# Scores and sign bits in fp16 halves for three of four batches, theta's product in fp16, and a new order of issue

## The chip, the cores and the metric

One core of one Trainium2 chip runs the whole program. The metric is the device time of one execution in microseconds. Seven engines or queues matter below: TensorE (PE, with its weight loads PEld), VectorE (DVE), ScalarE (ACT), GpSimd (POOL) and the SyncE queue (SP), which issues every DMA.

## The reference

Attention over 4 batches, 8 heads, 768 tokens and head size 64, with a mask from random projections, and a mixing layer on its output:

```python
q_bits = (q @ proj > 0); k_bits = (k @ proj > 0)          # 6 bits a token
mask   = bucket(q_bits)[:, None] == bucket(k_bits)[None, :]
scores = where(mask, q @ k.T / 8, -1e9)
x      = softmax(scores) @ v                              # heads side by side: 4 x 768 x 512
theta  = x @ w_theta                                      # 512 x 512
y      = w_tok_r @ (x * cos(theta)) + w_tok_i @ (x * sin(theta))   # 768 x 768, over tokens
u      = x + y
out    = u + max(u @ w_ch, 0)
```

Everything is asked for in float32. A product on TensorE reads operands with fewer bits, so each operand is written as a high part and a low part and a product is three matmuls (high by high, high by low, low by high).

## The kernel before, in words

**Pairs and steps.** Two heads of a batch form a pair; there are 16 pairs, 4 a batch. A pair is prepared once (`prep_qk`, line 601) and then gone through in 6 steps of 128 queries (`step`, line 687), so 24 steps a batch and 96 in all. When the heads of batch b are through, `moe(b, ...)` does the mixing layer of that batch, while the steps of batch b+1 run.

**Preparing a pair.** Queries and keys (`nat`, 128 rows by 768, two buffers, line 614) are loaded by DMA. ACT copies them to `hl` as fp32r (line 621, op `qkh`); DVE or POOL takes the low part by a subtraction (line 628, `qkl`). TensorE multiplies them with the projections `pst` (`bits`, line 642: four matmuls of 512 columns, four of 256), ACT and DVE add up (lines 655, 658), DVE or POOL turns the sums into plus or minus 2^40 (line 661, `sign`), and three DMAs spread the sign rows into `rows` and `kb` (line 673).

**A step.** `scores` (line 696) sums, for each of two heads, three products of `hl` halves and one of the sign rows into PSUM: 8 matmuls a head, each over 64 rows of the array, 4 of 512 columns and 4 of 256. In batches 1 to 3 the two heads' matmuls alternate, one on the array's upper and one on its lower rows (`st`); in batch 0 the heads go one by one. DVE takes the row maximum (line 722) and two small values (725, 728), ACT the exponential `pf` (732), ACT its fp16 copy (738), POOL the fp16 low part (744, `p2`), a DMA on SP transposes both (748), and TensorE multiplies with v (`pv`, 18 matmuls a head). In batch 0, one head of each two is instead transposed on TensorE (772) and multiplied in fp32 (`pv4`). There are two PSUM slots for scores, and one step takes both.

**The mixing layer.** For each of 6 token tiles of a batch: transpose (872), high part on ACT (877), low part on DVE (881), theta's product in fp32r (`project`, 4 times three matmuls of 512 columns), ACT and DVE for its fraction of a turn (913, 916, 919), sine and cosine on ACT (938, 939), then f, z high and z low (950, 955 or 957, 961) on DVE, ACT and POOL. Then 6 times 36 fp16 matmuls of 512 columns (`y`), and again transpose, split and product with `w_ch` in fp32r (`r`).

**Weights.** The weights come in as float64 and are narrowed on DVE, ACT and POOL; `split_weight` (430) makes the fp32r halves of w_theta and w_ch, `prep_wtok` the fp16 halves of the token matrices, `join_wtok` (495) brings their maxima to all partitions by a transpose and a matmul.

**Order.** Every operation is an `op` with a priority, the engines it may run on with a duration for each, its dependencies and its buffer slots. `issue_all` (127) goes through a model of the engines and writes out one fixed order for each engine. Where the model sees TensorE idle before its time 190 us, it puts in a matmul on constants (`fill`, 342). Priorities come from the numbers at the end of the file (KX, KY, W0, QK0 and so on). On the chip each engine then works through its list in order.

**Maxima of v.** `prep_v` already finds a power of two for v in each pair: maximum over the free axis on DVE (547), a DMA that turns the column into a row (550), a maximum of it (553), a DMA that spreads it (556), three small operations for the power of two (389 to 391), and a scaled fp16 copy on ACT (573) with the low part on DVE (582).

Of the kernel before, what the change touches and what calls it, by code (L numbers as in the profile page):

```python
# [31 lines left out]
def lsh_attention_moe_kernel(ctx: ExitStack, tc: tile.TileContext, qk, wt, v, consts, w_theta, w_ch, out):  # L32
# [86 lines left out]
    FREE = dict(nat=2, vr=1, wst=2, vv=2, x=2, z0=1, z1=1, xt=2, **BUFS, s=2, w=1, m=4)  # L119
# [262 lines left out]
    wth = [wp.tile([P, NC, DM], F32R, name=f"wth{i}") for i in range(2)]  # L382
# [5 lines left out]
    def pow2_scale(amax, inv, s):  # L388
        DVE.tensor_scalar(inv, amax, 1e-30, 2.0**-13, ALU.max, ALU.mult)
# [38 lines left out]
    wst_last = []  # L428

# [65 lines left out]
    def join_wtok(prio):  # L495
        t = {}
        sa = Slot("m")

        def own():
            DVE.tensor_reduce(wall, wam, AX.X, ALU.max)  # L500

        def tr():
            t["pa"] = bank(sa, [P, 2, P], "pa_w")
            PE.transpose(t["pa"][:1, 0], wall, ident)

        def row():
            t["a1"] = ap_.tile([1, 1], F32, tag="a1" + sa.tag, bufs=1, name="a1_w")
            DVE.tensor_reduce(t["a1"], t["pa"][:1, 0], AX.X, ALU.max)

        def everywhere():  # L510
            mm(t["pa"][:, 1, :2], t["a1"].to_broadcast([1, P]), ones1, True, True)
# [7 lines left out]
        o = op("wall", prio, on("DVE", 110, own), wamax)  # L519
        o = op("vall", prio, on("PE", 110, tr), [o], [sa])  # L520
        o = op("vall", prio, on("DVE", 198, row), [o], [sa])
        o = op("vall", prio, on("PE", 308, everywhere), [o], [sa])
# [73 lines left out]

# [90 lines left out]
    def step(g, b, hp, i, t, vt, po):  # L687
# [23 lines left out]
        for j in range(2):  # L711
            def head(j=j):
# [14 lines left out]
                def shift():  # L727
                    DVE.tensor_scalar(col(2), col(0), SHIFT, col(1), ALU.add, ALU.mult)  # L728
# [309 lines left out]
SEP = 24  # L1038
# [107 lines left out]
```

## Time and profile before

| | |
|---|---|
| runs shown | 787.96, 790.18, 927.24 us, median 790.18 us |
| profiled execution | 790.58 us, its span 788.8 us, granted clock 0.995 |
| PE busy | 757.3 us (96%), 6881 matmuls |
| DVE busy | 571.3 us (72%) |
| ACT busy | 535.4 us (68%) |
| POOL busy | 427.1 us (54%) |
| mean share of the DMA engines | 64.5% |
| chain that ended last | PE 71%, DVE 12%, ACT 8%, issue 4%, DMA 3% |

The span goes from the first to the last instruction; 1.8 us of the execution lie around it. Matmuls overlap and the end of each is modelled, so what a matmul costs is read from the distance of starts, not from its duration. A chain of waits is followed back from the end of a stretch: at each instruction to what released it, or to the one before it on its engine.

### The profile page before, as it was taken

The numbers are of one execution on the slowest core, as the hardware profiler recorded it, in microseconds if no ns is written. First come the engines' busy times: TensorE is split into PE (matmuls) and PEld (weight loads), VectorE is DVE, ScalarE is ACT, GpSimd is POOL, SyncE is SP. The second block draws the span as 40 slices with busy tenths as digits, with TensorE's granted clock in tenths as the row PEclk, the third lists the DMA queues.
The fourth block names the chain that finished last, engine by engine and source line by source line (L and its number), as shares of the span: only waits on it lengthen the run. The fifth ranks groups of instructions, "written<-read, shape, count | busy, mean of one in ns | idle before, by whom it ended". The sixth has DMA issues, their size and how long they took to land.

```text
span 788.8 us, 17523 instructions
## 1 busy us (share of the span) xinstructions
PE 757.3 (96%) x6881; PEld 537.5 (68%) x6881; DVE 571.3 (72%) x1218; ACT 535.4 (68%) x709; POOL 427.1 (54%) x309
## 2 busy tenths in 40 slices
PE   7999999999798999999999999999999999999998
PEld 3778878788565666777756666677666666666456
DVE  5887878888888787687996666787995665546223
ACT  3796867778898676668996666569966655658101
POOL 5465552646678586455666666465574654433200
PEclk9999999999989999999999999999999999999999
DMA  6357757666556898889349899784489876750002
GB/s 206 114 128 199 153 155 162 165 146 138 100 98 147 173 186 160 188 173 169 73 87 197 174 181 182 156 174 102 83 164 175 143 152 132 147 105 1 0 1 81
DMA packets 285283, 107.84 MB, mean 137 GB/s; under 512 B 270288, under 2 KB 274384, under 8 KB 285200
## 3 DMA queue, kind: packets, MB, share of 16 engines
q1 hardware_dynamic: 285200, 106.71, 64.1%
q8 instruction: 54, 0.88, 0.4%
q14 instruction: 29, 0.24, 0.1%
HBM read 32.54 MB, written 6.29 MB: 49 GB/s over the span
## 4 chain that ended last, share of the span: by engine, by line
PE 71%; DVE 12%; ACT 8%; issue 4%; DMA 3%; POOL 1%; SPq 0%; ACTq 0%; DVEq 0%; POOLq 0%
PE ps L84 67%; DVE mc L722 4%; ACT pf L732 2%; PE ps L772 2%; PE ps L872 2%; ACT pp L738 2%; DMA pt<-pp 1%; DMA nat<-in_qk_dram 1%; DVE rows L661 1%; ACT L732 1%; ACT z L955 1%; ACT n L913 1%; DMA wst<-in_wt_dram 1%; DVE sum L658 1%; DVE z L961 1%
## 5 line engine op out<-in xcount | busy, mean ns | idle before, releaser
L744 POOL TENSOR_TENSOR pp<-pf,pp 128x768 f16<-128x768 f32 x168 | 283.0, 1699 | 213.3 <-ACT pp L738 167.5
L732 ACT ACTIVATE pf<-ps,mc 128x768 f32<-128x768 f32 x192 | 182.5, 988 | 124.3 <-DVE mc L728 100.2
L722 DVE TENSOR_REDUCE mc<-ps 128x1 f32<-128x768 f32 x192 | 177.3, 951 | 91.6 <-PE ps L84 88.3
L84 PE MATMUL ps<-z,wtk 128*128 128x512 f16 x864 | 204.0, 379 | 0.1
L84 PE MATMUL ps<-hl 64*128 64x512 f32 (+1 forms) x1152 | 184.0, 354 | 9.6 <-ACT pf L732 9.5
L84 PEld LDWEIGHTS ps<-hl 64*128 64x128 f32 x1152 | 124.2, 186 | 56.5 <-ACT pf L732 26.8
L84 PE MATMUL ps<-vv,pt 128*128 128x65 f16 (+2 forms) x3312 | 155.0, 201 | 2.5 <-DMA pt<-pp 1.6
L738 ACT ACTIVATE pp<-pf 128x768 f16<-128x768 f32 x168 | 134.5, 839 | 0.5
L84 PEld LDWEIGHTS <-wtk 128*128 128x128 f16 x864 | 77.5, 98 | 79.8 <-issue 1.3
L84 PEld LDWEIGHTS <-pt 128*128 128x128 f16 x3024 | 105.9, 97 | 31.3 <-issue 11.3
L84 PE MATMUL ps<-kb,rows 64*128 64x256 f32 (+1 forms) x384 | 89.8, 335 | 0.0
L961 POOL TENSOR_TENSOR z<-f,z 128x512 f16<-128x512 f32 x31 | 41.0, 1330 | 50.1 <-ACT z L955 31.6
L84 PE MATMUL ps<-wch,h_u 128*128 128x512 f32 x192 | 66.2, 426 | 0.3
L84 PE MATMUL ps<-wth,h_x 128*128 128x512 f32 x192 | 63.3, 411 | 0.9 <-DVE wall L514 0.5
L84 PEld LDWEIGHTS ps<-kb,rows 64*128 64x128 f32 x384 | 53.0, 186 | 5.2
L950 DVE SCALAR_TENSOR_TENSOR f<-x,zr,z 128x512 f32<-128x512 f32 x48 | 46.6, 997 | 7.1 <-ACT z L938 4.9
L877 ACT ACTIVATE h_u<-ps 128x512 fp32r<-128x512 f32 x24 | 14.2, 594 | 51.1 <-PE ps L872 46.8
L84 PEld LDWEIGHTS ps<-wch,h_u 128*128 128x128 f32 x192 | 34.8, 189 | 9.4 <-ACT h_u L877 0.5
L84 PE MATMUL ps<-wch,l_u 128*128 128x512 f32 x96 | 38.2, 398 | 2.9 <-DVE l_u L881 2.9
L84 PEld LDWEIGHTS ps<-wth,h_x 128*128 128x128 f32 x192 | 34.8, 192 | 8.7 <-DVE l_x L881 0.8
L84 PE MATMUL ps<-wth,l_x 128*128 128x512 f32 x96 | 38.5, 401 | 0.6 <-DVE l_x L881 0.6
L84 PE MATMUL ps<-idle 128*128 128x512 f16 x126 | 33.7, 403 | 4.8 <-DVE sum L658 3.3
(115 smaller groups left out, 962.0 us busy)
## 6 DMA issues: line engine op xcount, KB each, us to landing
nat<-in_qk_dram SPq DMA_DIRECT2D x32, 384.0 KB
wst<-in_wt_dram SPq DMA_DIRECT2D x12, 768.0 KB
vb<-in_v_dram SPq DMA_DIRECT2D x16, 384.0 KB
out_dram<-x SPq DMA_DIRECT2D x24, 256.0 KB
pt<-pp SPq DMA_TRANSPOSE x168
w_th<-in_moe_w_theta_dram SPq DMA_DIRECT2D x4, 512.0 KB
w_ch<-in_moe_w_ch_dram SPq DMA_DIRECT2D x8, 256.0 KB
kb<-rows SPq DMA_DIRECT2D x32, 36.0 KB
```

The lines of the kernel that those rows point to most:

```text
L84: PE.matmul(out_, l, r, start=start, stop=stop, skip_group_check=True)
L658: DVE.tensor_tensor(u["s"], u["pb"][:56, :n_], u["s"], ALU.subtract)
L661: return lambda: eng.tensor_scalar(t["rows"][:56, lo : lo + n_], u["s"], affs[:56, 0:1], affs[:56, 1:2], ALU.is_ge, ALU.mult)
L722: DVE.tensor_reduce(col(0), st[j], AX.X, ALU.max, negate=True)
L732: ACT.activation(u["pf"], st[j], AF.Exp, bias=col(2), scale=col(1))
L738: ACT.activation(u["pp"][:, 0], u["pf"], AF.Copy)
L744: return lambda: eng.tensor_tensor(u["pp"][:, 1], u["pf"], u["pp"][:, 0], ALU.subtract)
L772: PE.transpose(u["pw"][:, tt], u["pf"][:, ts(tt, P)], ident)
L872: PE.transpose(u["pt"][:, c], src()[:, c * P : (c + 1) * P], ident)
L877: ACT.activation(u["hi"], u["pt"], AF.Copy)
L950: DVE.scalar_tensor_tensor(u["f"], tl[b][:, tt], t["zr"][:, 2 * tt + r : 2 * tt + r + 1], t["zw"][r][:, tt], ALU.mult, ALU.mult)
L961: return lambda: eng.tensor_tensor(t["z"][r, 1][:, tt], u["f"], t["z"][r, 0][:, tt], ALU.subtract)
```

## The change

In batches 1 to 3 queries and keys are scaled by a power of two and kept as fp16 halves, as are the projections and the sign rows; theta's product takes x and w_theta as scaled fp16 halves in all batches. The scale of a pair comes from its maximum, by the way of v's: two maxima on DVE, a DMA to a row, a maximum, a DMA to all partitions, four small operations; the copy on ACT and the low part (now always on DVE) carry the scale. The softmax factor and the sine's scale undo it. w_theta's halves are made in `prep_theta`, with the maximum brought to all partitions through the helper `spread_max`, taken out of `join_wtok`. In batch 0 the scores stay in fp32r, and p2 may be put on DVE there. The durations that `issue_all` works with change for several operations that are not themselves changed (`st` of one head 1340 to 1590, `ptr` 650 to 700, `pv4` 1225 to 1340), and nearly all priorities are new.

```diff
-    idle_ = const.tile([P, 512], F16, name="idle")
+    idle_ = const.tile([P, P], F16, name="idle")
...
-            mm(bank(sl, [P, 512], "fill"), idle_[:, :P], idle_, True, True)
+            mm(bank(sl, [P, 4, P], "fill"), idle_, idle_.unsqueeze(1).to_broadcast([P, 4, P]), True, True)
...
-    wth = [wp.tile([P, NC, DM], F32R, name=f"wth{i}") for i in range(2)]
+    wth = [wp.tile([P, NC, DM], F16, name=f"wth{i}") for i in range(2)]
...
+    def prep_theta():
...
+                h_ = op("whigh", prio, on("DVE", 595, high), [l_], [sx, sz])
+                e = op("wabs", prio, on("ACT", 650, lambda: ACT.activation(t["f"][:, c], t["f"][:, c], AF.Abs, scale=1.0 / TWO_PI, accum_out=tham[:, c : c + 1])), [h_], [sz])
...
+        u, o, sa = spread_max(tham, am, prio, muls, "t")
+        o = op("thsc", prio, on("DVE", 550, scale), [o], [sa])
+        for c in range(NC):
+            h_ = op("wh", prio + 0.1 * c, on("ACT", 620, lambda c=c: ACT.activation(wth[0][:, c], t["f"][:, c], AF.Copy, scale=thsc)), [o], [sz])
+            wready["th"] += [h_, op("wl", prio + 0.1 * c, on("DVE", 660, lambda c=c: DVE.scalar_tensor_tensor(wth[1][:, c], t["f"][:, c], thsc, wth[0][:, c], ALU.mult, ALU.subtract)), [h_], [sz])]
...
+        small = t["small"] = b > 0
+        dt = F16 if small else F32R
+        if small:
+            for i in range(2):
...
+                    ld = op("qkload", G + QKL + 0.02 * i, on("SP", [(330, 2 * S * D * 4)], load), slots=[sn])
+                    ams.append(op("qamax", pr, on("DVE", 860, lambda: DVE.tensor_reduce(qkam[:, 2 * n + i : 2 * n + i + 1], u["nat"], AX.X, ALU.max, apply_absolute_value=True)), [ld], [sn]))
...
+            o = op("qrow", pr, on("SP", [(560, P * 8)], lambda: dma(qkrow, qkam[:, two])), ams, [srow])
+            o = op("qone", pr, on("DVE", 330, lambda: DVE.tensor_reduce(qkone, qkrow.rearrange("o (p i) -> o i p", i=2), AX.X, ALU.max)), [o], [srow])
+            o = op("qbc", pr, on("SP", [(560, P * 8)], lambda: dma(qkam[:, two], qkone.unsqueeze(1).to_broadcast([1, P, 2]))), [o], [srow])
...
+            scaled = op("qscale", pr, on("DVE", 520, scale), [o])
...
+                    hs.append(op("qkh", pr, on("ACT", 826, high("ACT")), [scaled, loads[i]], [sn, sh]))
+                    ls.append(op("qkl", pr, on("DVE", 930, lambda: DVE.scalar_tensor_tensor(t["hl"][:, 1, i], u["nat"], qksc[:, 2 * n + i : 2 * n + i + 1], t["hl"][:, 0, i], ALU.mult, ALU.subtract)), [hs[-1]], [sn, sh]))
...
-            sts = [op("st", g + DJ * j, on("PE", 1340, lambda j=j: scores([j])), t["ready"], [ss[j]] + t["slots"]) for j in range(2)]
+            sts = [op("st", g + DJ * j, on("PE", 1590, lambda j=j: scores([j])), t["ready"], [ss[j]] + t["slots"]) for j in range(2)]
...
-            sts = [op("st", g, on("PE", 1600, lambda: scores([0, 1])), t["ready"], ss + t["slots"])] * 2
+            sts = [op("st16" if t["small"] else "st", g, on("PE", 1310 if t["small"] else 1600, lambda: scores([0, 1])), t["ready"], ss + t["slots"])] * 2
...
-                    k1 = op("ptr", gj + KX, on("PE", 650, across), [e], [spf, sw])
+                    k1 = op("ptr", gj + KX, on("PE", 700, across), [e], [spf, sw])
...
-                    o_ = op("pv4", gj + KZ, on("PE", 1225, pv4), [k2] + po["wait"] + po["all"][:1], [spt, po["slot"], vt["slot"], sx])
+                    o_ = op("pv4", gj + KZ, on("PE", 1340, pv4), [k2] + po["wait"] + po["all"][:1], [spt, po["slot"], vt["slot"], sx])
...
-                o = op("proj", prio, on("PE", 703, go), (deps + wdeps) if o is None else [o], [sm_, sxt])
+                o = op("proj" if kind == "r" else "th", prio, on("PE", 703 if kind == "r" else 648, go), (deps + wdeps) if o is None else [o], [sm_, sxt])
...
-P2 = [[0, 999, ['POOL']]]
+P2 = [[0, 24, ['POOL', 'DVE']], [24, 999, ['POOL']]]
...
-GR1 = 0
+GR1 = 2
```

## Rows read from the trace of the kernel before

**Rows 1.** Busy time of each engine in stretches of the span (us from its start; length, then busy time and instructions of each engine, granted clock of TensorE, share of the DMA engines, GB/s):

```profile
24.00:200.00 176.00, 173.21 (x1463) 141.13 (x1461) 147.11 (x328) 136.00 (x181) 93.60 (x68) 1.00 0.62 150
200.00:260.00 60.00, 53.20 (x455) 35.54 (x456) 52.35 (x103) 51.82 (x72) 41.18 (x29) 0.94 0.60 125
260.00:380.00 120.00, 117.97 (x1222) 84.69 (x1221) 90.23 (x204) 85.08 (x118) 75.60 (x54) 1.00 0.87 168
380.00:420.00 40.00, 38.52 (x362) 25.01 (x362) 37.82 (x63) 35.51 (x45) 26.22 (x19) 1.00 0.57 109
420.00:540.00 120.00, 117.39 (x1287) 83.68 (x1286) 85.24 (x197) 77.92 (x102) 71.84 (x49) 1.00 0.87 175
540.00:580.00 40.00, 38.83 (x318) 26.17 (x317) 37.87 (x69) 37.95 (x49) 25.79 (x17) 1.00 0.43 81
580.00:705.00 125.00, 120.12 (x1315) 83.94 (x1312) 73.75 (x186) 74.87 (x96) 67.56 (x46) 1.00 0.79 153
705.00:788.80 83.80, 78.84 (x388) 47.24 (x387) 33.24 (x46) 24.85 (x35) 11.18 (x8) 1.00 0.05 19
```

**Rows 2.** The chain of waits by line, one row for each of the first seven of these stretches, in their order (24:200, 200:260, 260:380, 380:420, 420:540, 540:580, 580:705):

```profile
by line: PE ps L84 74.9%; PE ps L772 9.6%; DMA wst<-in_wt_dram 3.2%; DVE mc L722 3.0%; DVE wtk L477 1.6%; issue 1.2%; DVE rows L661 1.0%; ACT pt L778 0.9%; DVE vv L582 0.8%; DVE l_x L881 0.7%; ACT pf L732 0.6%; DVE sum L658 0.5%; DVE wf_th 
by line: PE ps L84 25.0%; issue 14.0%; ACT pf L732 9.1%; ACT pp L738 5.3%; POOL z L961 5.0%; DVE f L950 4.7%; ACT L732 4.3%; ACT z L955 4.2%; POOL pp L744 3.4%; DVE mc L722 3.4%; DVE z L961 3.3%; ACT L938 2.1%; POOL wch L443 2.0%; ACT z L93
by line: PE ps L84 66.6%; DVE mc L722 6.9%; issue 5.7%; ACT pf L732 2.6%; ACT pp L738 1.9%; DVE x L822 1.8%; PE ps L872 1.7%; DVE rows L661 1.6%; DVE wf_ch L423 1.4%; DVE l_x L881 1.1%; ACT n L913 1.1%; ACT L732 1.1%; DVE mc L728 0.9%; DVE 
by line: DMA pt<-pp 15.1%; DVE mc L722 10.8%; ACT pp L738 10.5%; DVE z L961 7.9%; ACT pf L732 7.4%; issue 5.9%; ACT z L955 5.5%; ACT L732 5.0%; ACT n L913 4.9%; DVE z L919 4.5%; PE ps L84 3.5%; DVE f L950 3.4%; DVE l_x L881 3.0%; DVE vv L58
by line: PE ps L84 86.3%; DVE mc L722 4.5%; DVE rows L661 2.8%; PE ps L872 2.6%; DVE l_u L881 1.0%; DVE sum L658 0.9%; issue 0.8%; DVE x L989 0.6%; DVE mc L728 0.4%; DVE mc L725 0.3%; DVEq L658 0.0%; DVEq L722 0.0%
by line: PE ps L84 64.2%; ACT pf L732 4.7%; DVE z L919 4.5%; ACT pp L738 3.7%; ACT n L913 3.5%; issue 3.4%; ACT L732 3.2%; ACT z L955 2.6%; DVE mc L722 2.2%; ACT z L939 2.1%; ACT sum L655 1.6%; DVE l_x L881 1.5%; DVE rows L661 1.4%; ACT z L
by line: PE ps L84 77.1%; issue 5.1%; DVE mc L722 4.4%; DMA pt<-pp 4.1%; ACT pf L732 2.4%; PE ps L872 2.4%; ACT pp L738 1.3%; SPq L748 0.8%; DVE mc L725 0.6%; DVE mc L728 0.5%; DVE l_u L881 0.5%; DVE sum L658 0.3%; DVE rows L661 0.3%; ACT s
```

**Rows 3.** The row maxima of line 722 in the three stretches around the batch boundaries, two for each step (length, DVE busy and count, clock, DMA share, GB/s):

```profile
200.00:260.00 60.00, 11.22 (x12) 0.94 0.60 125
380.00:420.00 40.00, 8.19 (x9) 1.00 0.57 109
540.00:580.00 40.00, 7.73 (x9) 1.00 0.43 81
```

**Rows 4.** Matmuls in order of time (start us, duration us; a row merges alike instructions). Cost is start to next start: scores of one step, 512-column bits and v's product after them; 256-column bits and the next scores; three rounds of theta; 111 matmuls of y:

```profile
419.49 0.96 PE L84 MATMUL ps<-hl 64*128 64x512 f32 x6
...
421.09 1.20 PE L84 MATMUL ps<-hl,pst 128*128 128x512 f32 x4
422.13 0.73 PE L84 MATMUL ps<-vv,pt 128*128 128x65 f16 x18
...
500.53 0.82 PE L84 MATMUL ps<-hl,pst 128*128 128x256 f32 x4
501.27 0.96 PE L84 MATMUL ps<-hl 64*128 64x512 f32 x6
...
532.84 0.63 PE L84 MATMUL ps<-wth,h_x 128*128 128x512 f32 x2
...
533.54 0.63 PE L84 MATMUL ps<-wth,h_x 128*128 128x512 f32 x2
...
739.65 24.12 PE L84 MATMUL ps<-z,wtk 128*128 128x512 f16 x111
763.61 1.04 PE L872 MATMUL ps<-ident,x 128*128 128x128 f32 x8
```

**Rows 5.** Way of v's maximum in the pair whose load lands before 342.58: maximum on DVE, DMA to a row, DMA to all partitions, first small operation (start us, duration us; SPq is the queue on SyncE):

```profile
342.58 0.94 DVE L547 TENSOR_REDUCE vam<-vb 128x1 f32<-128x768 f32 x1
...
344.07 0.53 SPq L550 DMA_DIRECT2D vrow<-vam  x1
...
349.40 0.55 SPq L556 DMA_DIRECT2D vamax<-vone  x1
...
351.88 0.15 DVE L389 TENSOR_SCALAR vinv<-vamax 128x1 f32<-128x1 f32 x1
```

**Rows 6.** Prices by line: the low part of queries and keys on DVE (whole span: shortest, median, longest ns, first and last start) and, between 200 and 705 us (count, busy us, mean ns, idle before), on POOL; the scaled low part of v and the low part of z on DVE; the scaled fp16 copy of v on ACT:

```profile
L628 DVE TENSOR_TENSOR hl<-nat,hl x15: 948/1453/2290, 4.8 to 617.7; 128x768 fp32r<-128x768 f32 x15
...
L628 POOL TENSOR_TENSOR hl<-nat,hl 128x768 fp32r<-128x768 f32 x9 | 18.2, 2023 | 0.0
...
L582 DVE SCALAR_TENSOR_TENSOR vv<-vb,vsc,vv 128x768 f16<-128x768 f32 x10 | 10.1, 1006 | 0.0
L961 DVE TENSOR_TENSOR z<-f,z 128x512 f16<-128x512 f32 x13 | 19.7, 1518 | 1.5 <-ACT z L955 1.4
...
L573 ACT ACTIVATE vv<-vb,vsc 128x768 f16<-128x768 f32 x10 | 9.3, 929 | 3.2 <-PE ps L84 3.2
```

**Rows 7.** One pair's load of `nat` (issue on SP, start us, duration us) and ACT's first copy of it:

```profile
279.62 0.83 SPq L614 DMA_DIRECT2D nat<-in_qk_dram  x1
...
314.41 0.84 ACT L621 ACTIVATE hl<-nat 128x768 fp32r<-128x768 f32 x1 [0.52 <-PE ps L84]
```

**Rows 8.** The filling matmuls between 24 and 200 us (length, busy and count on PE, PEld, DVE, then clock, DMA share, GB/s):

```profile
24.00:200.00 176.00, 19.83 (x76) 7.05 (x74) 0.00 (x0) 1.00 0.62 150
```

**Rows 9.** Ten us after the first batch boundary (columns as in rows 1):

```profile
210.00:220.00 10.00, 7.00 (x61) 5.37 (x61) 8.44 (x18) 9.96 (x13) 6.41 (x4) 0.74 0.54 117
```

More of the change, by code (lines that the diff above doesn't have):

```diff
@@ L428, in lsh_attention_moe_kernel, with spread_max, tr, row @@
     wst_last = []
+    tham, thinv, thsc = (const.tile([P, n], F32, name=nm) for nm, n in (("tham", NC), ("thinv", 1), ("thsc", 1)))
+    txs = const.tile([P, 4 * B], F32, name="txs")
+    def spread_max(own, dst, prio, deps, nm):
+        t = {}
+        sa = Slot("m")
+        def tr():
+            t["pa"] = bank(sa, [P, 2, P], "pa_" + nm)
+            PE.transpose(t["pa"][:1, 0], dst, ident)
+        def row():
+            t["a1"] = ap_.tile([1, 1], F32, tag="a1" + sa.tag, bufs=1, name="a1_" + nm)
+            DVE.tensor_reduce(t["a1"], t["pa"][:1, 0], AX.X, ALU.max)
+        def everywhere():
+            mm(t["pa"][:, 1, :2], t["a1"].to_broadcast([1, P]), ones1, True, True)
+        o = op("wall", prio, on("DVE", 110, lambda: DVE.tensor_reduce(dst, own, AX.X, ALU.max)), deps)
+        o = op("vall", prio, on("PE", 110, tr), [o], [sa])
+        o = op("vall", prio, on("DVE", 198, row), [o], [sa])
+        o = op("vall", prio, on("PE", 308, everywhere), [o], [sa])
+        return t, o, sa
@@ L495, in join_wtok @@
     def join_wtok(prio):
[L496 to L511, printed above, removed]
+        t, o, sa = spread_max(wam, wall, prio, wamax, "w")
         def rel():
@@ L517, in rel @@
             DVE.tensor_scalar(wrel, winv, t["x"], 0.5, ALU.mult, ALU.mult)
[L519 to L522, printed above, removed]
         return op("wrel", prio, on("DVE", 600, rel), [o], [sa])
+    NSET = B * NP
     W1 = D + 1
@@ L640, in signs @@
                 u = {}
+                pst_ = pst_small if small else pst
                 def bits():
@@ L671, in spread @@
         def spread():
-            r_, k_ = (t[nm].bitcast(F32) for nm in ("rows", "kb"))
+            r_, k_ = (t[nm] if small else t[nm].bitcast(F32) for nm in ("rows", "kb"))
             dma(k_[:NM], r_[32 : 32 + NM])
@@ L675, in spread @@
             dma(k_[64 : 64 + NM], r_[32 + NM : 32 + 2 * NM])
-        sp = op("spread", G + at("QK1", b) + early + AB, on("SP", [(730, NM * S * 4)] * 3, spread), fs, [sr])
+        sp = op("spread", G + at("QK1", b) + early + AB, on("SP", [(730, NM * S * (2 if small else 4))] * 3, spread), fs, [sr])
         t["ready"], t["slots"] = hs + ls + [sp], [sh, sr]
@@ L689, in step @@
         smc = Slot("mc")
-        apart = g < SEP
+        apart = g < min(SEP, H * NQ)
         ss = [Slot("s"), Slot("s")]
@@ L862, in acc @@
             return sl, make
+        tsc, tmag, tfac = (txs[:, 4 * b + n : 4 * b + n + 1] for n in (1, 2, 3))
         def transposed(src, nm, prio, deps, kind):
+            small = kind == "x"
             u = {}
```

261 lines of the change are left out of this document (182 added, 79 removed).

## The prediction

> **What bounds the kernel now.** I read first the busy time by stretches [rows 1], then the chain of waits of the same stretches [rows 2], and only then single matmuls. The reader is to see three kinds of time in rows 1. From 24 to 200 us (batch 0) and in the long stretches 260 to 380, 420 to 540 and 580 to 705 PE is busy nearly throughout, DVE at 84% in batch 0 but at 59 to 75% in the long ones. Around the batch boundaries (200 to 260, 380 to 420, 540 to 580) DVE is busy for 128.0 of 140 us and ACT for 125.3. From 705 us on PE works almost alone. The chain says the same more sharply [rows 2]: PE holds 84.5% of it in batch 0 and 68%, 89% and 80% in the long stretches, but 25%, 4% and 64% around the boundaries. So a matmul made shorter is worth about its full saving in the long stretches and in the tail, and little at the boundaries, where 30 row maxima, so 15 of the 72 steps of batches 1 to 3, lie: 6, 4.5 and 4.5 [rows 3].
>
> **Scores.** A step of batches 1 to 3 costs 421.09 - 419.49 = 1.60 us [rows 4]. It has 4 pairs of 512 columns and 4 of 256, and the two heads' matmuls of a pair run beside each other. An fp16 matmul of 512 columns over all 128 rows costs (763.61 - 739.65) / 111 = 0.216 us, so 4 x 0.216 + 4 x 0.108 = 1.30 us would be such a step at the rate of y. No row shows fp16 scores over 64 rows: the bounds are 1.30 (rate of y) and 1.60 (no gain). I take 1.30, since y is the nearest fp16 stream and 1.60 is only 0.3 above it. Saving 0.30 a step.
>
> **Bits.** A pair's products cost 422.13 - 421.09 = 1.04 us for 512 columns and 501.27 - 500.53 = 0.74 for 256 [rows 4]; at y's rate 0.86 and 0.43. Saving 0.49 a pair, 0.08 a step. Together 0.38 a step.
>
> **Theta.** Three matmuls cost 533.54 - 532.84 = 0.70 us in fp32r, 0.65 at y's rate: 0.05 x 4 x 24 tiles = 5.0 us.
>
> **What of it counts.** The other 57 steps give 57 x 0.38 = 21.7, by the long stretches' mean share of the chain (79%) 17.1 us. The 15 give 6 x 0.38 x 0.25 + 1.71 x 0.04 + 1.71 x 0.64 = 1.7. Theta lies around the boundaries and in the tail; I count half, 2.5. Sum 21.3 us; at full credit 32.4.
>
> **What is added, DVE.** For each of 12 pairs: two maxima at 0.94 [rows 5], four small operations at 0.15, a maximum on one partition (between 0.15 and 0.94; 0.3, since it has 256 values alone), two scaled low parts at 1.01, the price of v's [rows 6]: 4.8 us. Gone are low parts at 1.45 that lay on DVE, some 12 of its 15, and at least 9 on POOL at 2.02 each. In sum 58 - 17 + 3 (six small operations at each batch's start) = 44 us more on DVE, so 377 + 44 = 421 of the 485 us that would be left between 200 and 705: 87%. In the long stretches this is hidden by matmuls; around a boundary, where one pair is prepared, it is not: 4.8 + 0.9 - 1.45 = 4.3 us, three times 12.8. POOL, relieved of 18.2 us, can take the 13 low parts of z (19.7 us) that DVE does [rows 6]. Bounds 0 and +12.8; I take +3, nearer to 0, since both amounts match.
>
> **ACT, SP, the round trip.** 24 copies with a scale at 0.93 [rows 6] for 0.84 [rows 7]: 2 us, beside matmuls; at a boundary at most 0.2. The 24 small DMAs hold SP for 0.54 each, 13 us in all, and stand ahead of transposes; SP must wait for the two maxima first, and behind it queue the transposes and so v's products. The way of a maximum through two DMAs took v 351.88 - 343.52 = 8.4 us [rows 5], 9 with the small operations. It stands between a load and ACT's copy, and there 34.8 us passed [rows 7], so I cost it at nothing; without that cover it would be 12 x 9 = 108 us. Scaled splits of x, the sine's scale and w_theta's new split I cost at nothing on PE; on DVE the low parts of w_theta add at most 4 x 1.6.
>
> **Batch 0 and the order.** The 76 fillers [rows 8] take 76 x 0.216 = 16.4 us of a stretch in which PE holds the chain. The planner put them where it thought PE idle, with 1340 ns for one head's scores where the new list has 1590, so part of them stands in the way; fewer are to be expected. But DVE, 147 of 176 us, gets some 10 us more there (w_theta's low parts, the projections, the first pair of batch 1). Bounds -16.4 and +10; I take -3, near the middle. Other changes of priority cannot be priced from rows: at nothing, inside the same bounds.
>
> **The sum.** The profiled execution took 790.58 us, 1.8 of it around the span, 0.4 over the median of 790.18. 790.6 - 21.3 - 3 + 3 = 769.3, so 769 us. Late next are DVE at the boundaries and the transposes: the DMA engines' 0.87 in the long stretches becomes about 0.91.
>
> **A rule that speaks against it.** The low parts of queries and keys on DVE vary from 0.95 to 2.29 us [rows 6], for one shape. The Trainium skill, "SBUF — State Buffer", section "Who interferes with whom", says that a DVE instruction with two SBUF inputs and a GpSimd instruction that reads SBUF block each other for a whole instruction; the spread of that row agrees, while v's scaled low part, also with two SBUF inputs, averages 1.01.
>
> **Rivals.**
> (1) *Better.* POOL takes the z parts, boundaries grow by nothing, PE's savings count in full and most fillers go: 790.6 - 32.4 - 12 = 746. For it: PE's share of the chain; against: DVE at 87% and its maxima in every step's loop.
> (2) *DVE at the boundaries.* The long stretches give half (8.6), the boundaries take 12.8 in full, nothing else is won: 790.6 - 8.6 - 1.7 - 2.5 + 12.8 = 791. If PE then also falls to half clock for longer, as at 210 to 220 us (granted 0.74, PE busy 7.0 of 10 us) [rows 9], 2.6 us a boundary more: 798. For it: DVE's 91% there.
> (3) *The port.* Each new low part takes 2.29 instead of 1.01; two a boundary add 2.6 us, in all 7.7: 777. Against: the mean of v's. The rule of the Trainium skill's page named above would have it so if every one met a running POOL instruction.
> (4) *It does not do what it says.* If fp16 scores stay at 1.60, 57 x 0.30 x 0.79 + 1.2 = 14.7 us are missing: 784.
> (5) *Slower.* SP's in-order queue. Each of the 24 small DMAs waits at the head for DVE, and transposes wait behind it. It decides when the wait outlasts the slack of two steps' transposes in the four buffers; v's small DMA waited 0.55 us after its maximum (344.07 - 343.52) [rows 5]. At 1.7 us of lost PE time each, 41 us: 769 + 41 = 810. Against: the loads lie 35 us ahead, so the order has room.
>
> **How the numbers follow.** Chances: forecast 0.58 (its own range 757 to 780), better 0.11, DVE 0.10, port 0.06, no gain in scores 0.07, slower 0.08. Two per cent, about what a measurement of this kernel tells from no change, are 774.4 and 806.0. Of the forecast about 0.46 lies below 774.4: faster 0.46 + 0.11 = 0.57; same 0.12 + 0.10 + 0.06 + 0.07 = 0.35; slower 0.08. The range from 746 to 790 leaves out half of the better case, the slower one and the upper part of the DVE case, together some 0.19.
>
> **What would show it.** In the profile after: scores of a step 1.30 apart, not 1.60; theta's three 0.65; DVE near 420 us between the first boundary and the tail, with low parts of z gone to POOL; fewer than 76 fillers; the boundary stretches no longer than 60 + 40 + 40 us. I am wrong if these stretches grow by more than a few us, if v's products begin to wait for transposes that wait for a small DMA, or if batch 0 takes longer than 200 us.

## The result, and the profile after

The changed kernel takes **798.96 us** in the median of 20 runs (793.24 to 839.54), the kernel before 791.75 in the median of 20: a ratio of 1.0053, 95% interval 1.0032 to 1.0074. It is slower by half a per cent: by its interval that is clear of no change, but it is under two per cent. Predicted were 769 us and a range from 746 to 790. The ratios here compare undisturbed runs only, a median takes in all; the changed kernel's median is raised by runs of a lower granted clock, of which more below.

The profiled execution took 801.34 us. Busy time of the engines, the granted clock in 40 slices, and the engines' shares of the chain that ended last:

```profile
span 799.6 us, 17616 instructions
PE 745.2 (93%) x6849; PEld 470.2 (59%) x6849; DVE 620.9 (78%) x1360; ACT 540.5 (68%) x712; POOL 407.7 (51%) x304
PEclk9996899999989999999899999999999999999999
PE 57%; DVE 23%; ACT 8%; DMA 6%; issue 4%; SPq 0%; POOL 0%; ACTq 0%; DVEq 0%; POOLq 0%
```

Before, PE was busy for 757.3 of 788.8 us, DVE for 571.3, and PE held 71% of the chain. So PE does 12 us less work (part of it at a lower clock), but its idle time goes from 31.5 to 54.4 us, and DVE has 50 us more to do. The same stretches as in [rows 1], with their ends moved along with the batches:

```profile
24.00:206.00 182.00, 170.89 (x1370) 138.26 (x1369) 158.74 (x365) 131.88 (x176) 83.41 (x62) 0.94 0.64 145
206.00:266.00 60.00, 50.56 (x455) 27.32 (x455) 54.42 (x105) 51.31 (x67) 35.81 (x23) 0.91 0.48 103
266.00:390.00 124.00, 119.38 (x1301) 71.88 (x1300) 105.83 (x244) 84.28 (x120) 77.88 (x60) 1.00 0.87 175
390.00:430.00 40.00, 33.21 (x303) 17.95 (x302) 35.48 (x69) 37.45 (x45) 21.33 (x15) 0.91 0.52 106
430.00:552.00 122.00, 118.95 (x1299) 70.28 (x1298) 97.49 (x231) 82.54 (x106) 71.44 (x50) 1.00 0.88 166
552.00:590.00 38.00, 31.43 (x326) 17.61 (x325) 36.36 (x70) 35.97 (x45) 26.13 (x19) 1.00 0.55 106
590.00:715.00 125.00, 121.37 (x1340) 72.40 (x1336) 84.52 (x204) 78.98 (x99) 66.36 (x45) 1.00 0.78 147
715.00:799.60 84.60, 79.49 (x385) 44.01 (x381) 34.74 (x49) 26.27 (x38) 8.75 (x7) 0.99 0.05 19
```

Read PE's busy time (170.89 in the first row) against the length before it (182.00). In batch 0 PE now lacks 11 us where it lacked 2.8; around the three boundaries it lacks 9.4, 6.8 and 6.6, where it lacked 6.8, 1.5 and 1.2; in the three long stretches together 11.3, where it lacked 9.5. For batch 0 and the first two boundaries the clock column says 0.94, 0.91 and 0.91 where it said 1.00, 0.94 and 1.00. The chain of the first stretch, against the first of [rows 2]:

```profile
by line: PE ps L82 41.7%; DVE mc L854 11.3%; DMA pt<-pp 7.5%; PE ps L910 4.4%; issue 3.9%; ACT pf L870 3.2%; DVE pt L918 2.5%; DVE wst L547 2.3%; DVE qkam L715 1.9%; DVE wst L544 1.7%; DVE wth L503 1.7%; DVE mc L866 1.6%; DVE x L960 1.4%; D
```

PE's share of it falls from 84.5 to 46.1%; the row maxima on DVE rise from 3.0 to 11.3%, transposes of probabilities come in with 7.5%. What PE waited for in the whole span (us, times, longest), first before, then after:

```profile
PE ps L84 <- ACT pf L732: 9.5, 16, 2.7
...
PE ps L84 <- DMA pt<-pp: 1.6, 3, 0.9
```

```profile
PE ps L82 <- ACT pf L870: 17.4, 22, 2.7
PE ps L82 <- DMA pt<-pp: 16.9, 16, 3.4
```

That is 23 us more of waiting for the exponents and for their transposes. Not all of it goes with DVE's new work. The same two waits in two kernels of the experiments, first fp16 in the old order (*fp16, whole*), then the new order without the scaling (*no maxima*):

```profile
PE ps L93 <- ACT pf L747: 11.2, 17, 2.8
PE ps L93 <- DMA pt<-pp: 4.7, 10, 1.3
```

```profile
PE ps L82 <- DMA pt<-pp: 12.7, 12, 3.4
PE ps L82 <- ACT pf L870: 11.8, 19, 1.5
```

From 11.1 us before, the sum goes to 15.9, 24.5 and 34.3: by single profiles some 5 us come with fp16, 9 with the new order, 10 with the scaling. Fillers between 24 and 206 us are 35, not 76 [rows 8].

The prices of the shorter matmuls (start and duration; cost from start to next start):

```profile
441.22 0.82 PE L82 MATMUL ps<-hl 64*128 64x512 f16 x6
...
442.62 0.73 PE L82 MATMUL ps<-wch,h_u 128*128 128x512 f32 x2
...
509.24 0.72 PE L82 MATMUL ps<-hl,pst 128*128 128x256 f16 x4
509.89 0.82 PE L82 MATMUL ps<-z,wtk 128*128 128x512 f16 x3
...
540.12 0.59 PE L82 MATMUL ps<-wth,h_x 128*128 128x512 f16 x2
540.55 0.38 PE L82 MATMUL ps<-wth,l_x 128*128 128x512 f16 x1
540.76 0.59 PE L82 MATMUL ps<-wth,h_x 128*128 128x512 f16 x2
...
545.76 1.80 PE L82 MATMUL ps<-hl,pst 128*128 128x512 f16 x8
547.50 0.66 PE L1019 MATMUL ps<-ident,x 128*128 128x128 f32 x4
```

A score step costs 1.40 us, 0.20 less than in [rows 4], not 0.30; bits of 512 columns 0.87 (two groups in 1.74), as predicted, those of 256 columns 0.65, not 0.43; theta's three 0.64, as predicted.

**The granted clock.** Where the clock fell, in stretches of 10 us (columns as in [rows 1], the clock third from the end):

```profile
50.00:60.00 10.00, 8.92 (x63) 5.93 (x62) 9.24 (x18) 8.60 (x11) 7.12 (x5) 1.00 0.96 236
60.00:70.00 10.00, 8.53 (x63) 7.34 (x61) 9.42 (x21) 6.56 (x10) 6.50 (x4) 0.89 0.46 146
70.00:80.00 10.00, 10.00 (x43) 8.85 (x41) 3.78 (x10) 5.84 (x9) 3.97 (x3) 0.50 0.42 86
80.00:90.00 10.00, 10.00 (x75) 8.70 (x74) 5.58 (x12) 4.29 (x7) 2.79 (x3) 0.76 0.49 94
...
220.00:230.00 10.00, 6.84 (x74) 3.83 (x72) 9.93 (x23) 9.96 (x15) 6.83 (x4) 1.00 0.39 73
230.00:240.00 10.00, 8.31 (x64) 4.35 (x65) 9.74 (x11) 7.69 (x11) 7.48 (x5) 0.66 0.19 37
240.00:250.00 10.00, 7.72 (x52) 3.60 (x50) 8.10 (x17) 8.62 (x10) 3.34 (x3) 0.83 0.68 168
```

A clock of 0.50 is 1.2 GHz instead of 2.4. Ahead of each fall PE was thin: 8.9 and 8.5 of 10 us, then 6.8. In the changed kernel time follows the clock of the run: 793.5 us at 0.987, 801.3 at 0.976, 814.6 at 0.958, 839.5 at 0.927. A straight line through its 20 runs falls by 7.4 us a hundredth, one through 55 runs of before by 7.8. So a time can be moved to an equal clock at 7.7 us a hundredth; a kernel's runs, moved so to 0.985, keep a standard deviation of 1 to 2 us. There the kernel before would be at 799 (798.7 to 799.5 in its seven sets of runs) and the changed one at 795. The change saves 4 us at equal clock, and loses 11 by the lower clock. The kernel before can lose its clock too: one of its runs took 1068.63 us at 0.639, which the same rate brings to 802, and of its first 20 runs two, at 927.24 and 1494.52 us, have no clock on record.

### The profile page after: what moved, and what is told of

It reads as the page before. It is cut to its first block, busy times and chain, and to the rows that moved or that the text cites. A ratio compares the mean times of both kernels' runs of the same rounds, so it can differ in the third digit from the quotient of the medians.

```text
span 799.6 us, 17616 instructions
## 1 busy us (share of the span) xinstructions
PE 745.2 (93%) x6849; PEld 470.2 (59%) x6849; DVE 620.9 (78%) x1360; ACT 540.5 (68%) x712; POOL 407.7 (51%) x304
## 4 chain that ended last, share of the span: by engine, by line
PE 57%; DVE 23%; ACT 8%; DMA 6%; issue 4%; SPq 0%; POOL 0%; ACTq 0%; DVEq 0%; POOLq 0%
PE ps L82 55%; DVE mc L854 7%; DMA pt<-pp 4%; ACT pf L870 3%; DMA nat<-in_qk_dram 2%; ACT pp L876 1%; PE ps L1019 1%; DVE f L1104 1%; DVE qkam L715 1%; PE ps L910 1%; DMA vamax<-vone 1%; DVE l_x L1029 1%; DVE wst L547 1%; ACT L870 1%; DVE z L1070 1%
## 5 line engine op out<-in xcount | busy, mean ns | idle before, releaser
L82 PE MATMUL ps<-hl 64*128 64x512 f16 (+3 forms) x1152 | 175.2, 339 | 17.8 <-ACT pf L870 17.4
L82 PE MATMUL ps<-vv,pt 128*128 128x65 f16 (+2 forms) x3312 | 160.7, 204 | 17.7 <-DMA pt<-pp 16.9
L82 PE MATMUL ps<-kb,rows 64*128 64x256 f16 (+3 forms) x384 | 88.4, 333 | 0.0
L82 PEld LDWEIGHTS <-hl 64*128 64x128 f16 x864 | 43.3, 95 | 64.5 <-issue 40.0
L1115 POOL TENSOR_TENSOR z<-f,z 128x512 f16<-128x512 f32 x35 | 45.6, 1315 | 68.4 <-ACT z L1109 39.8
L82 PE MATMUL ps<-wth,h_x 128*128 128x512 f16 x192 | 58.8, 389 | 3.1 <-DVE l_x L1029 3.1
L82 PEld LDWEIGHTS ps<-hl 64*128 64x128 f32 x288 | 46.3, 191 | 17.3 <-ACT pf L870 7.2
L82 PEld LDWEIGHTS ps<-vv,pt 128*128 128x128 f32 x288 | 37.0, 206 | 2.8 <-DVE sum L790 0.6
L82 PE MATMUL ps<-wth,l_x 128*128 128x512 f16 x96 | 37.1, 386 | 0.0
L1143 DVE SCALAR_TENSOR_TENSOR x<-ps,sw,x 128x512 f32<-128x512 f32 x24 | 17.4, 743 | 24.6 <-PE ps L82 24.5
```

Of the source, the lines that this page charges most:

```text
L82: PE.matmul(out_, l, r, start=start, stop=stop, skip_group_check=True)
L1115: return lambda: eng.tensor_tensor(t["z"][r, 1][:, tt], u["f"], t["z"][r, 0][:, tt], ALU.subtract)
L1143: DVE.scalar_tensor_tensor(tl[b][:, to], res["py"], t["sw"], tl[b][:, to], ALU.mult, ALU.add)
```

## The experiments

Theory ORDER: the saving is real, and the new written order gives it back in waits of PE. Rivals: VectorE's new work does it; the way over the two small transfers does it; the clock alone does it. All runs in one table (4 to 20 of each kernel but before, which has more; median; ratio to before with its interval; granted clocks; mean of the runs moved to a clock of 0.985):

| kernel | order | median us | ratio | clock | at 0.985 |
|---|---|---|---|---|---|
| before | old | 791.75 | | 0.980 to 0.998, once 0.639 | 799 |
| changed | new | 798.96 | 1.0053 (1.0032 to 1.0074) | 0.927 to 0.987 | 795.3 |
| old numbers | third | 848.87 | 1.0769 (1.0684 to 1.0854) | 0.940 to 0.966 | 827.5 |
| small maxima | new | 803.56 | 1.0106 (1.0036 to 1.0175) | 0.951 to 0.984 | 793.3 |
| fp32r halves | new | 811.62 | 1.0239 (1.0182 to 1.0295) | 0.964 to 0.983 | 800.8 |
| no scale, replanned | fourth | 835.51 | 1.0508 (1.0437 to 1.0579) | 0.929 to 0.958 | 807.2 |
| no maxima | new | 795.93 | 0.9997 (0.9951 to 1.0042) | 0.924 to 0.988 | 786.3 |
| no dependency | new | 794.59 | 1.0033 (0.9997 to 1.0069) | 0.966 to 0.986 | 792.6 |
| no transfers | new | 805.91 | 1.0082 (1.0038 to 1.0126) | 0.936 to 0.982 | 790.4 |
| one wide | new | 800.86 | 1.0033 (1.0005 to 1.0060) | 0.960 to 0.989 | 791.8 |
| double fillers | new | 823.02 | 1.0390 (1.0337 to 1.0444) | 0.941 to 0.971 | 809.0 |
| fp16 | old | 781.01 | 0.9860 (0.9810 to 0.9910) | 0.993 to 0.995 | 788.4 |
| fp16, whole | old | 782.55 | 0.9891 (0.9837 to 0.9945) | 0.991 to 0.995 | 788.4 |
| theta alone | old | 790.36 | 0.9999 (0.9976 to 1.0022) | 0.989 to 0.996 | 796.8 |
| low halves on DVE | old | 786.76 | 0.9945 (0.9914 to 0.9975) | 0.990 to 0.996 | 792.7 |
| DVE's work, no transfers | old | 811.05 | 1.0230 (1.0175 to 1.0285) | 0.971 to 0.977 | 802.4 |
| whole scaling | old | 822.39 | 1.0327 (1.0269 to 1.0384) | 0.965 to 0.989 | 811.0 |

**Old numbers.** The changed code with the old order numbers (theta's due times alone put where the new code can be ordered), so the planner writes a third order:

```diff
-KX = 21.947
+KX = 3.346
...
-TH1 = 0.882
+TH1 = 0.307
```

> The changed kernel with the priorities of the kernel before (KX to Y1, P2 on POOL alone, GR1 0); w_theta's chunks keep their priorities but in rising order, since the new preparation needs it. Theory ORDER (the new set of priorities costs the time): 770 to 782 us, batch 0 back at 160 us or less. Theory DVE (the added vector work eats the gain whatever the order): 793 to 810 us, DVE busy near 620 us.

Measured 848.87 us, outside both ranges. The old numbers do not fit the new list of operations; that an order is kept with its numbers was a wrong idea, and this run tells only how far numbers reach.

**Small maxima.** The same order, the maxima over 8 of 768 columns:

```diff
-DVE.tensor_reduce(qkam[...], u["nat"], ...)
+DVE.tensor_reduce(qkam[...], u["nat"][:, :8], ...)
```

> The changed kernel in its own order to the instruction; the 24 maxima of queries and keys go over 8 of 768 columns, so that some 19 to 20 us leave DVE and nothing else changes. Leaves out: 760 of 768 columns of each maximum. Theory DVE: 6 to 15 us faster than the changed kernel (780 to 790 us). Theory ORDER: within 3 us of it (792 to 799 us).

The median is no better; at equal clock 2.0 us are won (four runs, good to about 1 us), of 16 us less on DVE: within 3 us, as theory ORDER had it. The maxima's length is mostly hidden in this order.

**fp32r halves.** The same order and the same added work, but halves and sign rows in fp32r:

```diff
-        dt = F16 if small else F32R
+        dt = F32R
```

> The changed kernel in its own order, scaled as it is, but the halves of queries, keys, projections and the sign rows of batches 1 to 3 are fp32r again. If the matmuls of scores are on the path at their full saving (72 x 0.20 us + bits): 12 to 17 us slower than the changed kernel (807 to 814 us). If TensorE waits for DVE anyway: 0 to 6 us slower.

5.5 us over the changed kernel at equal clock, the 0 to 6 of a TensorE that waits for DVE; the median is 12.7 higher, but by runs of a lower clock. So fp16 scores and bits are worth 5.5 us in the new order. In the old one they are worth 8.4 (788.4 for fp16, 796.8 for theta alone).

**No scale, replanned.** Maxima, transfers and scale out of the list of operations:

```diff
-            srow = Slot("qr")
...
-            scaled = op("qscale", pr, on("DVE", 520, scale), [o])
```

> The changed kernel without maxima, round trips and scales of queries and keys: plain fp16 halves, the low part on DVE or POOL as before; the order is planned anew from the same priorities. Leaves out the scaling of queries and keys. Theory DVE: 765 to 782 us, DVE busy 575 to 590 us. Theory ORDER: 788 to 800 us though DVE has as little to do as before.

Less work, and 835.51 us, outside both ranges although DVE's busy time is the 579 us that theory DVE named: the planner's fourth order is worse by more than all the work left out. Only orders held fixed can be compared, so the next runs change what the instructions do and leave the list alone.

**No maxima.** The new order, instruction by instruction, with maxima, transfers and scale arithmetic emptied:

```diff
-on("DVE", 520, scale)
+on("DVE", 520, lambda: None)
...
-AF.Copy, scale=qksc[:, 2 * n + i : 2 * n + i + 1])
+AF.Copy, scale=2048.0)
```

> The order of the changed kernel, instruction by instruction, but the 24 maxima, the 24 small transfers, the reductions of the 256 values and the scale's arithmetic are left out; the halves are scaled by the constant 2048. Theory ORDER (the time is lost where the written order makes TensorE wait for transposes and exponents, not in the maxima): 792 to 802 us, TensorE's idle time stays near 59 us. Rival CHAIN (the way from a load over the maxima and the two small transfers to the halves is late and holds up batches 1 to 3): 775 to 786 us. Rival ADDED WORK (VectorE's 30 us of new instructions count where they stand): 780 to 788 us.

The profiled run took 783.37 us at 0.988, where the changed kernel takes 793.5 at 0.987: 9 to 10 us less, inside the ranges of both rivals. The median, 795.93 us, lies in theory ORDER's range, since the runs reach down to a clock of 0.924; PE's idle time is 45 us in the profile, not near 59. At equal clock the new order without the scaling (786.3) is no slower than the old one (788.4), so that theory holds only by way of the clock.

**fp16 in the old order.** The old list and order; halves, sign rows and theta's product in fp16, unscaled, so nothing is added. The sign rows held values too small for their mask, so this kernel leaves out a working mask:

```diff
-t["hl"] = ap_.tile([P, 2, 2, S], F32R, ...)
+t["hl"] = ap_.tile([P, 2, 2, S], F16 if b else F32R, ...)
...
-wth = [wp.tile([P, NC, DM], F32R, ...
+wth = [wp.tile([P, NC, DM], F16, ...
```

> The order of the kernel before, instruction by instruction (its planner sees the old durations and the old set of operations), but the halves of batches 1 to 3, the sign rows and theta's product hold fp16; no maximum and no scale is taken, so nothing is added. Theory ORDER (the matmuls' saving is real and the new order gives it back): 773 to 781 us, that is 791.8 less 0.2 us a score step in 57 steps, 0.2 us in 24 groups of bits, and 0.05 us in 96 threes of theta's, 11.4 + 4.8 + 5 = 21 us in full, or two thirds of it where a step ends on TensorE. Rival CUSHION (shorter matmuls only turn TensorE's work into waits, in whatever order, and its clock falls for it): 786 to 796 us, with TensorE's idle time up by 10 us or more.

```profile
PE 738.9 (95%) x6881; PEld 463.7 (60%) x6881; DVE 570.0 (73%) x1218; ACT 535.2 (69%) x709; POOL 426.6 (55%) x317
```

PE's work falls by 18.4 us (from 757.3), the span by 10.4 (788.8 to 778.4), and the clock stays at 0.995. This is what fp16 alone brings: 57% of what it takes off PE.

**fp16, whole.** The same with sign rows of plus and minus 2 to the 15th:

> The kernel of the fp16 halves in the order of before, now with sign rows of plus and minus 2 to the 15th as the changed kernel has them; the halves are not scaled, so it leaves out the scaling from the maximum. Theory ORDER: as that run, 778 to 784 us, granted clock 0.993 or more in all runs, since no gap of the changed kernel's order is in it. Rival: values of full size in the sign rows change nothing of the time, so any other time would be the disagreement of two sets of runs.

782.55 us, ratio 0.9891: 1.1% faster than the kernel before. It leaves out the scaling, so it holds only for inputs whose halves fit fp16's range as they are.

**Theta alone**, fp16 in the old order:

> The order of before, theta's halves alone in fp16, everything else as before. By the prediction's price (0.05 us off each three of theta's 96 after the first, half of it on the path) 1 to 4 us under the kernel before, ratio 0.995 to 0.999; if the 10.5 us of the run with fp16 in both came from theta's part in the main, 0.988 to 0.993; if shorter matmuls of theta's only lengthen waits, 1.000 or above.

Ratio 0.9999, though PE's busy time falls from 757.3 to 752.6; at equal clock 2 us are won (796.8 against 799). The medians show nothing, and 2 us are near the limit of what equal clocks show.

**No dependency.** Every added instruction in the new order stays, but the halves and the factor use constants:

```diff
-AF.Copy, scale=qksc[:, 2 * n + i : 2 * n + i + 1])
+AF.Copy, scale=2048.0)
...
-t["factor"] = qkf[:, n : n + 1]
+t["factor"] = 2.0**-20 * 0.25 / math.sqrt(D)
```

> Every instruction of the changed kernel in its order, the 24 maxima, the small transfers and the scale's arithmetic among them, but the halves are scaled by the constant 2048 and the factor of the exponents is a constant, so that nothing reads the computed scale. Left out is only that use. Beside the kernel without maxima (783.4 us at a granted clock of 0.988; the changed kernel 793.5 at 0.987), this splits the 10 us. Theory WAIT (the way from a load over the maximum and two small transfers to the halves is late): 782 to 786 us at a clock of 0.985 or more. Rival ADDED WORK (VectorE's small operations and the queue's small transfers cost where they stand): 792 to 796 us at that clock.

792.6 at equal clock: of the 9 us, 2.7 hang on using the scale. The waits of the halves for it are not the main cause.

**No transfers**, on top of that:

> The kernel whose halves do not depend on the scale, and of it the 24 small transfers (the row of 256 maxima in, the two results out) are left out as well; VectorE's maxima and scale instructions all stay in the changed kernel's order. Beside the kernel without a dependency (793 us at a clock of 0.986 to 0.982) and the kernel without maxima, transfers and scale (783.4 at 0.988): theory QUEUE (a small transfer waits in the in-order queue for VectorE, and the transposes behind it start late): 784 to 788 us at a clock of 0.985. Rival VECTORE (43 us of new instructions on VectorE, 22 of them maxima, stand ahead of the maxima and factors of the softmax): 791 to 794 us at that clock.

790.4 at equal clock, between the two ranges: the transfers are worth some 2 us, VectorE's instructions the other 4. Such steps are good to about 1 us.

**Double fillers.** Each filler's matmul twice:

> The changed kernel in its order, but each of its 88 filler instructions is issued twice (0.2 us each, 18 us of TensorE's time if all of it counted), half of them while batch 0's attention runs. Theory CLOCK (the scatter of the changed kernel from 793 to 839 us comes from stretches at half clock, which begin after thin stretches of TensorE): where fillers stand ahead of such a stretch, the clock of the worst runs rises over 0.97 and the median falls to 785 to 796 us with a scatter under 10 us. Rival PLACE (the stretches begin where no filler stands): the scatter stays, and the time rises by 3 to 18 us.

The worst result of the new order: 24 us more in the median, 14 at equal clock, and outside both ranges. Fillers stand in the way, and the clock falls all the same (0.941 to 0.971); as a cure this fails. What goes with the clock is seen by comparing kernels: those of the old order without the maxima kept 0.989 or more (before itself 0.980, but for its one run at 0.639), all others had runs under 0.973. So both the new order and the unplanned scaling bring lower clocks; that thin stretches are the way to it is argued from the rows above, not shown.

**Whole scaling in the old order.** Maxima, transfers and scale are put into each engine's stream behind a pair's second load; lower halves on DVE alone, as in the change:

```diff
                 NOW[0] = now
+                for ch in chains:
+                    while ch and ch[0][0] == e and ch[0][1] <= now:
+                        advance(ch, now)
                 fn()
```

> The changed kernel's matmuls and its scaling in the order of before: the order of the kernel of whole fp16 halves, and into each engine's stream, behind the second load of a pair and ahead of its halves, the two maxima, the two small transfers and the scale's instructions are put; the halves and the exponents' factor use the computed scale, and the lower halves stand on VectorE alone as in the changed kernel. Theta's halves stay unscaled, which leaves out only a scale that is taken once. Theory ADDED WORK (the new instructions cost 4 to 9 us wherever they stand, and the clock falls with the new order's thin stretches): granted clock 0.988 or more in all runs, 785 to 792 us, so at or a little under the kernel before and under the changed one. Rival ORDER ALONE (the new instructions are free where VectorE has room): 781 to 785 us. Rival DISTURBED (put in without a plan they stop the in-order queues at the turns of the batches): 795 to 806 us, clock under 0.985.

822.39 us, outside all three ranges: 40 over the run without scaling, 23 at equal clock. Its best run, 809.72 us, has a clock of 0.989, so it is not the clock in the main. Two runs take it apart.

> The kernel of the changed kernel's scaling in the order of before, without maxima, transfers and scale instructions: the halves are scaled by the constant 2048, the exponents' factor is a constant, and all lower halves of batches 1 to 3 stand on VectorE. Theory VECTORE (each microsecond on VectorE ahead of the softmax's maxima counts in part): 784 to 790 us, since only 12 of the lower halves (1.2 us each) are new there. Rival LOWER HALVES (the lower halves on VectorE are what stops the steps): 800 us or more. Rival TRANSFERS (only the waits for the small transfers count): 780 to 784 us.

> The kernel of the changed kernel's scaling in the order of before, with all of VectorE's new instructions, but without the 24 small transfers and with a constant in place of the computed scale. Theory VECTORE: 800 to 815 us, close to the run with everything (822.4). Rival TRANSFERS: 782 to 790 us, close to the run of whole fp16 halves (782.6). Rival LOWER HALVES: the time of the run that keeps the lower halves alone, to 3 us.

At equal clock the ladder is 788.4 (nothing), 792.7 (12 lower halves moved to DVE), 802.4 (24 maxima and the small instructions), 811.0 (transfers and the use of the scale): 4, 10 and 9 us. Here DVE does wait for a transfer at the head of its own queue, the softmax's maxima behind it:

```profile
DVE qkone L657 <- DMA qkrow<-qkam: 6.2, 5, 3.6
```

**One wide.** In the changed kernel one small instruction stands out. DVE and POOL at the second boundary (start, duration):

```profile
386.24 0.16 DVE L387 TENSOR_SCALAR qkinv<-qkam 128x2 f32<-128x2 f32 x1
386.44 3.46 DVE L388 TENSOR_SCALAR qkinv<-qkinv 128x2 uint32<-128x2 uint32 x1
386.63 3.24 POOL L882 TENSOR_TENSOR pp<-pf,pp 128x768 f16<-128x768 f32 x2
...
389.93 0.17 DVE L389 TENSOR_SCALAR qksc<-qkinv 128x2 uint32<-128x2 uint32 x1
390.01 0.21 DVE L727 TENSOR_SCALAR qkf<-qkinv 128x1 f32<-128x1 f32 x1
390.13 0.74 DVE L1070 SCALAR_TENSOR_TENSOR z<-n,txs,ps 128x512 f32<-128x512 f32 x1
390.79 1.81 DVE L854 TENSOR_REDUCE mc<-ps 128x1 f32<-128x768 f32 x2
```

A two-element instruction lasts 3.46 us and ends with POOL's two products; theta's remainder and the softmax's maxima stand behind it. The edit makes them one element wide:

```diff
-                pow2_scale(qkam[:, two], qkinv[:, two], qksc[:, two], 2.0**-8)
+                for c_ in (slice(2 * n, 2 * n + 1), slice(2 * n + 1, 2 * n + 2)):
+                    pow2_scale(qkam[:, c_], qkinv[:, c_], qksc[:, c_], 2.0**-8)
```

> The changed kernel in its order, but the three small instructions of a pair's scale, which work on two neighbouring values at once, are written as two times three instructions on one value. Theory STANDSTILL (an instruction on two neighbouring 32-bit values is stopped by a running product of GpSimd, one on a single value is not: v's same instruction lasted 0.153 to 0.156 us in all 16): the three forms last 0.14 to 0.21 us in every pair, VectorE's busy time falls by some 4 us, and the time at equal granted clock falls by 2 to 6 us (793 to 789 at 0.985, where the changed kernel is at 795). Rival LENGTH (VectorE's standstill is hidden): 794 to 796 us at that clock.

The instruction's shortest, median and longest time (ns), in the changed kernel and in this one:

```profile
L388 DVE TENSOR_SCALAR qkinv<-qkinv x12: 169/170/3462, 133.6 to 625.6; 128x2 uint32<-128x2 uint32 x12
```

```profile
L388 DVE TENSOR_SCALAR qkinv<-qkinv x24: 153/153/155, 127.5 to 613.4; 128x1 uint32<-128x1 uint32 x24
```

Twice as many instructions, none stopped, and 3.5 us less at equal clock, inside theory STANDSTILL's 2 to 6; the median, 800.86 us, is no better. Nor is it chance that none met a running product: of all 72 one-value instructions (three forms) 20 started while a GpSimd product ran, and none lasted over 0.156 us; of the changed kernel's 36 two-value ones 4 started so, and all four lasted 1.04 to 1.60 us, to the product's end. In the kernel of whole scaling 11 of 36 are stopped, so part of its cost is theirs. What PE gains is in its waits for the exponents (13.3 us, from 17.4); those for the transposes stay (17.0, from 16.9). The Trainium skill, "SBUF — State Buffer", section "Who interferes with whom", says that a tensor_scalar may use the ports that DVE shares with GpSimd, and that the two then block each other for a whole instruction. The trace agrees with the blocking, 3.46 us beside 3.24, though this one began 0.2 us ahead of the products that it waited for (starts on POOL are rough).

## Why the prediction was wrong

The median of 799.0 lies 29.7 us over the sum's 769.3. At equal clock, by the table, that splits into 10.6 us of fp16's saving that did not come (10.7 of 21.3), 6.0 of scaling beyond the 3 that were counted (9.0), 0.9 of the new order (2.1 won, 3 counted), 11 of the granted clock, which the sum had at nothing, and 1.1 of a starting value of 790.6 for 791.75. So three steps failed: the price of the matmuls, DVE at +3, and the clock.

**What bounds it** was read rightly, and so was what is late next, but not how little that left. PE held 84.5% of the chain in batch 0 [rows 2], while DVE had 29 us to spare there (147.1 of 176, [rows 1]); after it holds 46.1%, and DVE has 23 to spare.

**Scores and bits**: mis-sized. 0.30 a step was taken at y's rate [rows 4], 0.20 came; a pair's bits gave 0.26 (0.17 and 0.09) instead of 0.49. That rate was called the nearest, but it is one over 128 rows, and no row had fp16 over 64. (In rival 4 the 1.2 us should be 1.4, which leaves its 784.) **Theta**: right as a price (0.64); whether 2.5 us of it lie on the path is open, since alone it gave nothing in the median and 2 us at equal clock.

**What of it counts**: 21.3 us were counted, 10.4 came in the old order (profile against profile). With the measured prices the same step gives (0.20 + 0.26 / 6) x 57 x 0.79 = 11.0 and 1.1 at the boundaries, 12.1 without theta. So the share of the chain was a fair guide, and the prices were what failed.

**DVE at +3 us** is mis-sized. DVE's busy time came as counted (414 us between 206 and 715, predicted 421, by rows after; POOL took 5 of DVE's 13 low parts of z, not all). In the new order, which plans for them, the added instructions and transfers cost 9 us at equal clock (786.3 to 795.3). The same stretches without them (*no maxima*; the first boundary to the third long stretch):

```profile
198.80:258.80 60.00, 53.61 (x515) 29.14 (x515) 53.26 (x103) 54.33 (x71) 40.09 (x26) 0.94 0.54 110
258.80:376.40 117.60, 114.95 (x1241) 69.14 (x1242) 90.91 (x215) 81.93 (x117) 73.59 (x57) 1.00 0.89 180
376.40:416.40 40.00, 35.02 (x342) 19.00 (x341) 35.65 (x68) 39.75 (x50) 26.11 (x17) 1.00 0.52 110
416.40:534.60 118.20, 116.29 (x1276) 69.33 (x1273) 85.45 (x205) 77.57 (x101) 67.22 (x48) 1.00 0.86 170
534.60:572.60 38.00, 32.24 (x322) 18.01 (x318) 33.58 (x65) 36.25 (x46) 25.96 (x19) 0.96 0.50 104
572.60:697.20 124.60, 121.08 (x1334) 72.35 (x1334) 81.19 (x197) 78.38 (x98) 66.36 (x45) 1.00 0.80 148
```

With the scaling PE's idle time rises from 17.1 to 22.8 us at the boundaries, the place that the prediction named, and from 8.1 to 11.3 in the long stretches, for 30 us more of DVE's work there: most of it is hidden, as said, but not all. Put into the old order unplanned, the same work costs 23 us at equal clock, and in the long stretches 42 us more on DVE bring 18 more of idle time to PE (12.5 to 30.5). Of the 9 us some 4 are VectorE's instructions, 2 the transfers, 3 the use of the scale, which makes each of 144 factors 204 ns long instead of 147. Cutting across these, 3.5 come from two-element instructions that were priced at 0.15 and last up to 3.46.

**The round trip at nothing**: nearly right in the new order (2 us for the transfers), wrong for the old, where with the use of the scale it took 9. (The 34.8 us of cover count from the load's issue, not from its landing.) Rival 5 has the right place there, but not the price of 41: v's products do wait longer for transposes, but of the 16.9 us 11.3 stay without the small transfers.

**Batch 0 at -3** was about right, and the clock hides it. Between the batches' first maxima, in the kernel before, in the changed one, and in the one without a dependency, which has all of its instructions in its order:

```profile
22.20:182.10 159.90, 158.19 (x1309) 128.44 (x1307) 133.37 (x296) 125.34 (x167) 83.27 (x63) 1.00 0.63 153
22.70:187.90 165.20, 157.95 (x1243) 129.71 (x1241) 144.79 (x327) 119.53 (x160) 76.58 (x59) 0.95 0.62 145
24.10:182.00 157.90, 151.36 (x1249) 123.57 (x1248) 145.29 (x327) 119.91 (x163) 77.83 (x59) 1.00 0.66 152
```

At a clock of 1.00 it is 2.0 us shorter than before, with the fewer fillers and the some 10 us more on DVE that were forecast; in the profile of the changed kernel it ran in part at half clock and grew.

**The clock** stood in rival 2 alone, at 2.6 us a boundary. It is the largest single item of the result: 11 us between the usual runs of the two kernels. Rival 2 (791, with half clock 798) came nearest, with a chance of 0.10, but that its number fits is luck in part: batch 0 loses its clock too, and the scaling cost the boundaries less than 12.8. So the sum at equal clock reads 799.1 - 10.7 (fp16) - 2.1 (new order without maxima) + 9.0 (scaling) = 795.3, and the clock adds the rest. These are differences of runs, not parts proved independent.

**Still open** is what decides, from run to run, whether the clock falls after a thin stretch: without maxima PE was as thin from 50 to 70 us (8.6 and 8.6 of 10) and kept 1.00.

```profile
50.00:60.00 10.00, 8.62 (x79) 6.07 (x78) 6.70 (x16) 8.45 (x11) 8.16 (x5) 1.00 1.04 218
60.00:70.00 10.00, 8.55 (x59) 6.80 (x57) 9.20 (x20) 6.60 (x11) 5.73 (x5) 1.00 0.55 196
```

## What to carry to other kernels

Before work is moved from the busiest engine to the next, price the next one's microseconds in the loop that feeds the first: here 18 us less matmul were worth 10, and the scaling that came with them cost 9 in a good order and 23 in an unplanned one. Test a change of data type with the order held fixed, and take the version without the side work if the range of the data allows it: fp16 unscaled in the old order ran in 782.55 us. Compare runs at equal granted clock before explaining a difference of one per cent.

## What was unexpected of the hardware

A VectorE instruction on two neighbouring 32-bit values took 0.17 us or up to 3.46, by what GpSimd was doing; on one value it took 0.15 in all 24, and 20 of 72 such instructions began while a GpSimd product ran. One kernel's time follows its granted clock at 7.4 us a hundredth, from 793 to 840 us on one core with nothing else changed. fp16 scores of 64 rows, two heads beside each other, cost 1.40 us a step where the rate of 128-row matmuls gives 1.30.
